# Attention and gated feed-forward on one core: seven half products for half of gate and value, a residual added by transfers, and a listed order

## The chip, the core and the metric

The kernel runs on one core of a Trainium2 chip. A core has a matrix engine (TensorE, PE in the profile), a vector engine (DVE), an activation engine (ACT), a general engine (POOL) and a queue engine (SP); POOL and SP issue the transfers here. Matmul results go to PSUM, eight banks of 128 x 512 fp32. The metric is device time in microseconds, the median of three runs.

## The reference, cut to what is computed

The first stage is attention over 4 batches, 8 heads, 768 positions and 64 values per head. Heads 0, 2 and 6 are causal; the other five see only the first 4 positions and the last 64. The second stage takes the result as x, 3072 tokens of 512 features:

```python
x = np.ascontiguousarray(attn_out.transpose(0, 2, 1, 3)).reshape(B * S, H * D)
g = x @ w_gate                                    # 512 -> 1536
gelu = 0.5 * g * (1.0 + erf(g * inv_sqrt2))
val = x @ w_val                                   # 512 -> 1536
ffn_out = gelu * val @ w_out                      # 1536 -> 512
res_gate = 1.0 / (1.0 + np.exp(-(x @ w_res)))
return (x + res_gate * ffn_out).astype(np.float32)
```

## The kernel before

The 3072 tokens are worked in six chunks of 512, c = 0 to 5 (the constant CHUNKS, line 25); a chunk may span two batches. For every chunk there is an attention stage (scores, exponentials, masks, weighted values, a transpose to features), a gate/value stage and an output stage. Work of neighbouring chunks overlaps: while gate and value of chunk c run, the output of chunk c-1 and the scores of chunk c+1 are fitted in.

Nothing is written as a loop of instructions. Functions add tasks to a graph (class Graph, line 195), each with an engine, a duration, what it depends on, a priority and its buffers. Tasks are numbered in the order in which they are added. `schedule` (line 219) then plays time forward and lets each free engine take the ready task of lowest priority number; HINTS (line 46) overrides single priorities by task number. `assign_waits` turns dependencies into semaphore waits and `emit` writes each engine's instructions in the order found. An engine executes its list in order, so a waiting instruction holds up all behind it. A task that has two homes (`flex`, line 212) goes to DVE or ACT as time is played.

Buffers come from pools. `P_ot` is four tiles otile of 128 x 512 fp32, `P_sr` three srs; `P_ps` is PSUM, with a list of permitted banks and a number held at once for each kind of use.

Gate and value (`gate_value`, line 1121): for each f of 12 blocks of 128 hidden features, gate and value are four matmuls each, with a 128 x 128 block of wg or wv as weights and 512 tokens of xT moving. ACT applies gelu (line 1166), DVE multiplies gelu and value into hT (line 1168). c=0 works the first blocks in halves of 256 tokens.

The output stage (`output_fast`, line 1213; the first half of c=0 uses `output`) already multiplies hT and wo by seven half products for a pair of token tiles, pi = 0 or 1, with sums of hT (`sums`, line 1174, line 1187) and of wo (`weight_sums`, line 1199, line 1204) made on DVE. Partial results are copied (keep, lines 1251 and 1252) and added (plus, line 1257) in otile; gated (line 1281) multiplies by the residual gate; then DVE, or POOL in c=5, adds x (line 1286), and SP stores the tile (line 1292). For c=5, pi=1 is called `end`.

Each matmul goes through `mm` (lines 513 to 517): where the tiling of PE is by columns, it is issued as two halves of 64 columns of weights (line 517), otherwise whole (line 516). q and k are loaded by POOL (line 577) and, from c=2 on, transposed by SP's transfers into one tile qkt that holds q and k of a whole batch.

Of the kernel before, what the change touches and what calls it, by code (L numbers as in the profile page):

```python
# [4 lines left out]
NHEAD = 8  # L5
SEQ = 768
DHEAD = 64
# [36 lines left out]


HINTS = (
    "3:-58.9 11:-130.04 428:854.14 430:718.61 444:2782.08 457:-821.9 460:407.45 490:4205.68 521:1522.06 "
    "591:-818.43 610:-36.63 612:486.89 613:-2965.25 619:1544.03 621:-44.07 643:467.87 644:-881 646:4.3 656:119.6 "
    "664:25.04 673:629.62 675:-109.25 695:-2674.26 696:-1856.67 703:-881.5 706:-108.75 707:714.39 708:1939.7 "
    "711:270.02 712:497.18 716:476.22 720:652.56 738:638.32 743:520.23 744:3053.24 749:514.3 750:1799.28 "  # L50
    "751:2383.53 756:521.28 762:1469.72 764:4344.87 767:2237.74 787:-603.93 815:5053.25 817:2978.67 821:1231.87 "
    "824:1484.86 836:2402.62 837:798.1 841:706.04 848:-288.52 849:2997.07 876:2751.74 906:2555.54 913:1516.93 "
    "918:2437.99 919:1519.88 924:1537.25 931:1510.23 936:2384.32 949:2443.79 955:2089.28 967:2846.74 995:-227.38 "
    "1001:29.83 1002:3171.86 1003:3180.29 1004:1146.58 1007:2686.58 1012:1781.89 1040:-803.29 1043:1907.45 "
    "1045:1028.83 1046:667.33 1050:3229.28 1051:1536.45 1053:3573.03 1056:-1823.77 1084:4090.27 1110:2454.97 "
    "1111:2597.62 1117:2808.38 1123:2507.5 1128:2481.58 1129:2529.63 1134:2508.5 1146:2434.73 1152:2779.33 "
    "1153:3034.61 1158:3861.94 1165:2795.06 1171:3076.63 1176:2997.8 1185:5989.69 1188:2243.92 1189:2528.84 "
    "1192:2789.39 1193:2537.45 1194:3836.22 1208:3021.15 1215:6294.68 1263:3219.13 1268:5037.38 1283:4420.5 "
    "1308:4756.92 1311:3513.6 1317:3517.03 1321:3052.3 1329:5930.49 1330:3507.5 1335:3508.5 1336:3519.22 "
    "1341:4624.14 1345:3444.6 1353:3516.64 1354:3538.83 1357:2761.66 1365:3787.63 1366:5173.04 1372:5102.72 "  # L60
    "1386:5438.32 1392:4014.31 1393:4933.66 1418:5146.68 1430:4133.91 1441:5428.8 1452:5127.54 1457:2188.42 "
    "1462:4595.33 1464:5711.23 1467:9389.54 1468:4425.54 ~1471:550.69 1476:5611.77 1499:4504.13 1513:6742.83 "
    "1516:5340.27 1522:4510.5 1523:4585.63 1526:3632.38 1534:4503.02 1539:4253.34 1550:4463.64 1565:7711.51 "
    "1570:4506.5 1571:5085.34 1580:2427.42 1594:2466.44 1610:9272.71 1625:3048.93 1627:6036.71 1629:6167.81 "
    "1631:5064.12 1644:6476.5 1662:4125.72 1671:5044.95 1672:7314.6 1676:4967.2 1683:6427.71 1692:9540.12 "
    "1711:7387.16 1757:5137.62 1784:5507.1 1797:5469.41 1803:7562.23 1817:7773.49 1818:7478.69 1823:7672.83 "
    "1834:7419.08 1836:10250.4 1849:7490.55 "
)

# [121 lines left out]
VS_DMA = 0  # L191
LAT = {"pe": 0.20, "act": 0.10, "dve": 0.08, "pool": 0.12, "sp": 0.1}


class Graph:
# [22 lines left out]

    def schedule(self):
# [21 lines left out]
        running = []  # L241
        while left:
# [3 lines left out]
            for e in ENGS:  # L246
# [3 lines left out]
                for t in cand[e]:  # L250
# [6 lines left out]
                    key = (int(away), p_, t.seq)  # L257
                    if t.ready > now or (best is not None and key >= bkey):
                        continue
                    if t.alts and any(max(free[f], now) + t.alts[f][0] + BIAS[f] < now + t.alts[e][0] + BIAS[e] - 1e-6  # L260
                                      for f in t.alts if f != e):
                        continue
# [22 lines left out]
                progressed = True  # L285
                if t.name == "g0" and warming:
                    warming = False
                    cand["pe"] = [w for w in cand["pe"] if w.name != "warm"]
                    gone = [w for w in self.tasks if w.name == "warm" and w.end is None]
                    left -= len(gone)  # L290
                    self.tasks = [w for w in self.tasks if w not in gone]
# [109 lines left out]
    def emit(self):  # L401
# [31 lines left out]
        with nc.Block() as blk:  # L433
# [17 lines left out]
            @blk.sync  # L451
            def _(e):
                run("sp", e)
                for t in finals:
                    e.wait_ge(t.sem, 16)
# [6 lines left out]
def c_act(n):  # L462
    return 0.19 + n * 0.000834


def c_dve(n, rate=1.0, psum=True):
    return (0.125 if psum else 0.065) + n * 0.00104 / rate
# [6 lines left out]
def build_kernel(nc, q, k, v, w_gate, w_val, w_out, w_res, out):  # L474
# [11 lines left out]
    scratch = sb("scratch", [128, 1], FP16)  # L486
    blank = sb("blank", [128, 128], FP16)
# [4 lines left out]
    P_vs = Pool(many("vs", 2, [128, NT - 1, NHEAD, DHEAD + 1], FP16))  # L492
    P_vk = Pool(many("vk", 2, [128, 8, DHEAD + 1], FP16))
    P_qkt = Pool(many("qkt", 2, [128, 2, NPAIR, SEQ], FP16))
# [9 lines left out]
    P_hs = Pool(many("hS", 1, [128, 3, NF // 2, 2, 128], FP16))  # L504
    wt = sb("wt", [128, 4, NF // 2, 256], FP16)
    P_ga = Pool(many("gact", 4, [128, 512], FP16))
    P_sr = Pool(many("srs", 3, [128, 512], FP32))
# [5 lines left out]
    def mm(e, o, lhsT, rhs, **k):  # L513
# [8 lines left out]
        "gv": (4, one(6, 7, 5, 4, 3, 2)), "gv0": (4, one(6, 7, 5, 4)), "gvh": (4, one(7, 6, 4, 5)), "out": (2, one(6, 7)), "fin": (4, one(6, 7, 1, 0)), "warm": (1, one(7, 5)),  # L522
# [55 lines left out]

    wtok = {}

    def load_weights():
# [6 lines left out]
        for j in range(4):  # L588
# [3 lines left out]
            wtok["o", j].late = 2.2  # L592
        for nm in "gv":
            for j in range(3):
                wtok[nm, j].late = 2.2 if j else 2.0
# [8 lines left out]
    def batch(b):  # L604
        if b not in batches:
            B_ = B()
            B_.v, B_.vs, B_.vk, B_.qkt = Buf(P_v), Buf(P_vs), Buf(P_vk), Buf(P_qkt)
# [4 lines left out]
        return batches[b]  # L612

    def values(b, a, z, base, each, on_engines=False):

        BB = batch(b)
        for i in range(a, z):
            BB.vtok[i] = dma("pool", base, 0.9, (lambda i=i: lambda: at(BB.v)[:, i, :, 0:DHEAD])(),
                             v[b, :, i * 128:(i + 1) * 128, :].rearrange("h p d -> p h d"), bufs=[BB.v])
            BB.vtok[i].late = 1.6 if base < 50 else 6.0  # L620
        if a == 0:
# [9 lines left out]
            for t in BB.vktok:  # L631
                t.slack = 12.0 if b else 0.0
# [5 lines left out]
        if on_engines:  # L638
            ts = []
            for lo, hi, pr in ((1, 2, -75),) + (() if VS_DMA else ((2, 4, 130),)):  # L640
                for dst, src, off in ((0, 64, 1), (64, 0, 0)):
                    def vs(on, dst=dst, src=src, off=off, lo=lo, hi=hi):
                        def fn(e):
                            o = at(BB.vs)[dst:dst + 64, lo - 1:hi - 1, :, :].rearrange("p i h d -> p (i h d)")
                            i_ = at(BB.v)[src:src + 64, lo - off:hi - off, :, :].rearrange("p i h d -> p (i h d)")
                            return e.activation(out=o, in_=i_, func=AF.Copy) if on == "act" else e.tensor_copy(out=o, in_=i_)
                        return fn
                    n_ = (hi - lo) * 520
# [9 lines left out]
        for lo in cuts:  # L658
            hi = lo + 1 if each else z
            ts = []  # L660
            for dst, src, off in ((0, 64, 1), (64, 0, 0)):
                ts.append(G.add("sp", 1.2, (lambda lo=lo, hi=hi, dst=dst, src=src, off=off: lambda e: e.dma_start(
                    at(BB.vs)[dst:dst + 64, lo - 1:hi - 1, :, :].rearrange("p i h d -> p (i h d)"),
                    at(BB.v)[src:src + 64, lo - off:hi - off, :, :].rearrange("p i h d -> p (i h d)")))(),
# [7 lines left out]
    def loads_rows(c, si, b, a, z):  # L672
# [27 lines left out]
        per = 1 if c == 0 or n == 4 else 2  # L700
        for k_ in range(0, NPAIR, per):
            ps_ = ORDER[k_:k_ + per]
            pr = 1000 * c - 492 + ps_[0] if c else 40 * k_ - 205
            for js in (((1,), (0,)) if c == 0 else ((0, 1),)):
                scr = Buf(P_ps, "scr" if c else "scr0")
                items = [(p, jj) for jj in js for p in ps_]
# [10 lines left out]
                def ev(on, p0=ps_[0], scr=scr, j0=js[0], m=len(items)):  # L717
                    def fn(e):
                        o = at(BB.qkt)[:, :, :, lo:hi].rearrange("c j (y x) w -> c x (j y) w", x=2)[:, p0 % 2]
                        m0 = j0 * 2 + p0 // 2  # L720
                        o = o[:, m0:m0 + m, :].rearrange("c m (p j) -> c m p j", j=n)
# [5 lines left out]
                           bufs=[scr, BB.qkt], name="qkE")  # L727
# [4 lines left out]
    def loads_natural(c, si, b, a, z):  # L732
# [8 lines left out]
        for i in range(a, z):  # L741
            for j, src in ((1, k), (0, q)):
# [11 lines left out]
                t = G.add("sp", 1.65, (lambda sv=sv, i=i, j=j: lambda e: e.dma_start(  # L754
# [690 lines left out]
```

The softmax here doesn't subtract the row's maximum and nothing guards it: scores larger than these inputs give would overflow.

## Time and profile before

| what | value |
|---|---|
| median of three runs | 265.71 us (265.57 to 266.54) |
| span of the profiled execution | 263.7 us |
| ACT gelu, line 1166 | 68 of 597 ns |
| DVE product, line 1168 | 68 of 686 ns |
| output transfers on SP, issue to landing | 2.4 us (median) |
| loads of v on POOL, issue to landing | 17.6 us (median) |
| PE clock granted | 1.000 |

The span is that of one profiled execution; the runs are timed without a profile. In the profile a group line gives count, total busy time and mean length of one instruction, then the idle time of the engine before them and what ended it. In a table of windows each pair is busy time and number of instructions, for PE, PEld (weight loads), DVE, ACT and POOL, then clock, transfer share and GB/s.

### The profile page before, as it was taken

The page shows a single profiled execution, that of the slowest core. Times are in us where ns is not written, and L with a number is a line of the kernel's source. Part 1 is how long each engine was busy: PE and PEld are TensorE (multiplying, and loading weights), DVE is VectorE, ACT ScalarE, POOL GpSimd, SP SyncE. Part 2 cuts the span into 40 slices and gives each one's busy share as a digit, 9 for nine tenths or more (in the row PEclk, how much of TensorE's full clock was granted, in tenths as well). Part 3 has the DMA queues.
Part 4 walks back from the last instruction along what each step waited for, and adds up shares of the span by engine and source line. Part 5 has one row for each costly group of instructions (what it writes and reads, how often), then busy time and mean ns, then how long its engine had stood idle before and what let it go on. Part 6 is the DMA issues. An engine that isn't in the chain of part 4 may idle for free.

```text
span 263.7 us, 7495 instructions
## 1 busy us (share of the span) xinstructions
PE 257.7 (98%) x3226; PEld 164.0 (62%) x3226; DVE 181.6 (69%) x378; ACT 147.2 (56%) x237; POOL 89.3 (34%) x127
## 2 busy tenths in 40 slices
PE   7999999999999999999999999999999999999993
PEld 6777655468444668544567444589655588655692
DVE  2698437798447888557898366888557689837655
ACT  2785467974244987423787242967243888233430
POOL 8999979506109973975000000000000000000003
PEclk9999999999999999999999999999999999999999
DMA  6999999999999999999996110004200004200003
GB/s 83 174 204 206 188 175 231 175 153 204 134 200 148 165 137 177 171 179 176 174 156 150 42 40 0 2 26 101 82 2 0 2 2 122 82 2 0 2 35 127
DMA packets 96513, 29.22 MB, mean 111 GB/s; under 512 B 84449, under 2 KB 93025, under 8 KB 96481
## 3 DMA queue, kind: packets, MB, share of 16 engines
q0 software_dynamic: 70320, 14.69, 67.5%
q1 hardware_dynamic: 26160, 14.07, 28.0%
q8 instruction: 25, 0.41, 0.7%
q14 instruction: 8, 0.06, 0.1%
HBM read 29.36 MB, written 6.29 MB: 135 GB/s over the span
## 4 chain that ended last, share of the span: by engine, by line
PE 95%; DMA 2%; DVE 1%; issue 0%; POOLq 0%
PE ps L516 50%; PE ps L517 32%; PE ps L893 5%; PE ps L1333 2%; PE ps L1017 2%; PE ps L709 2%; DMA qks<-in_q_dram 2%; PE ps L1106 2%; PE ps L984 1%; DVE otile L1281 1%; DVE otile L1286 1%; DVE otile L1257 0%; POOLq L1427 0%
## 5 line engine op out<-in xcount | busy, mean ns | idle before, releaser
L1166 ACT ACTIVATE gact<-ps 128x512 f16<-128x512 f32 x68 | 40.2, 597 | 73.5 <-PE ps L516 43.7
L1168 DVE SCALAR_TENSOR_TENSOR hT<-gact,ps 128x512 f16<-128x512 f16 x68 | 46.1, 686 | 48.0 <-PE ps L516 23.1
L516 PE MATMUL ps<-xT,wg 128*128 128x512 f16 (+1 forms) x208 | 50.0, 363 | 0.0
L516 PE MATMUL ps<-xT,wv 128*128 128x512 f16 (+1 forms) x202 | 49.0, 362 | 0.0
L1286 POOL TENSOR_TENSOR otile<-otile,xtok 128x256 f32<-128x256 f32 x3 | 2.4, 801 | 136.2 <-DVE otile L1281 136.2
L577 POOL DMA_DIRECT2D qks<-in_k_dram x36 | 28.0, 810 | 17.3 <-DMA qkt<-qks 13.9
L516 PEld LDWEIGHTS ps<-xT,wg 128*128 128x128 f16 x208 | 20.1, 98 | 20.0 <-DVE otile L1257 0.3
L516 PEld LDWEIGHTS ps<-xT,wv 128*128 128x128 f16 x202 | 19.4, 98 | 20.0 <-DVE hT L1168 0.5
L577 POOL DMA_DIRECT2D qks<-in_q_dram x36 | 28.4, 828 | 2.2 <-issue 1.4
L517 PE MATMUL ps<-xT,wv 128*64 128x512 f16 x204 | 28.3, 380 | 0.0
L577 POOL DMA_DIRECT2D va<-in_v_dram x24 | 21.3, 920 | 15.1 <-PE ps L516 15.1
L517 PE MATMUL ps<-xT,wg 128*64 128x512 f16 x192 | 26.3, 379 | 0.0
L909 ACT ACTIVATE ea<-ps 128x1024 f16<-128x1024 f32 (+2 forms) x24 | 21.1, 915 | 1.7 <-PE ps L893 1.6
L1257 DVE TENSOR_TENSOR otile<-otile,ps 128x256 f32<-128x256 f32 x33 | 13.6, 417 | 7.1 <-PE ps L517 4.7
L1226 ACT ACTIVATE srs<-ps 128x512 f32<-128x512 f32 x22 | 13.1, 595 | 9.1 <-PE ps L517 6.7
L517 PEld LDWEIGHTS ps<-xT,wv 128*64 128x64 f16 x204 | 11.5, 110 | 9.8 <-DVE hT L1168 0.3
L1084 DVE TENSOR_TENSOR xtok<-ps,rcp 128x512 f32<-128x512 f32 (+1 forms) x28 | 16.8, 606 | 0.2
L517 PEld LDWEIGHTS ps<-xT,wg 128*64 128x64 f16 x192 | 11.1, 110 | 9.0
L893 PE MATMUL ps<-qkt 64*128 64x64 f16 (+4 forms) x391 | 16.4, 213 | 0.0
L893 PEld LDWEIGHTS ps<-qkt 64*128 64x128 f16 x391 | 9.8, 94 | 8.0 <-issue 4.2
L516 PE MATMUL ps<-wo,hT 128*128 128x256 f16 (+1 forms) x84 | 14.4, 304 | 0.0
L1286 DVE TENSOR_TENSOR otile<-otile,xtok 128x512 f32<-128x512 f32 (+1 forms) x21 | 14.3, 691 | 0.2
(109 smaller groups left out, 437.4 us busy)
## 6 DMA issues: line engine op xcount, KB each, us to landing
out_dram<-otile SPq DMA_DIRECT2D x22, 256.0 KB, 2.4
va<-in_v_dram POOLq DMA_DIRECT2D x24, 128.0 KB, 17.6
qks<-in_k_dram POOLq DMA_DIRECT2D x32, 64.0 KB, 12.6
qks<-in_q_dram POOLq DMA_DIRECT2D x32, 64.0 KB, 13.0
wg<-in_moe_w_gate_dram POOLq DMA_DIRECT2D x3, 512.0 KB, 10.2
wv<-in_moe_w_val_dram POOLq DMA_DIRECT2D x3, 512.0 KB, 12.1
wo<-in_moe_w_out_dram POOLq DMA_DIRECT2D x4, 384.0 KB, 22.8
vs<-va SPq DMA_DIRECT2D x4, 260.0 KB, 7.9
```

Source lines behind the costliest of these rows:

```text
L516: return e.matmul(o, lhsT=lhsT, rhs=rhs, **k)
L517: return [e.matmul(o[h:h + 64], lhsT=lhsT[:, h:h + 64], rhs=rhs, **k) for h in (0, 64)][-1]
L577: return G.add(eng, issue, lambda e: e.dma_start(out_ap(), in_ap), deps, prio, bufs=bufs, dma=cost, name=name, grp=grp)
L709: return [e.transpose(out=at16(scr)[64 * x:64 * x + 64, (m * n + i) * 128:(m * n + i + 1) * 128], in_=piece(jj, h, i), identity=ident[:, : ...
L893: return [e.matmul(at(scr)[:, oo:oo + w], lhsT=side(BB, low, 1)[half, k0:k0 + 128], rhs=side(BB, low, 0)[half, qq:qq + w], start=True, sto ...
L909: return e.activation(out=o, in_=i_, func=AF.Exp, scale=SM_SCALE)
L1084: t2 = G.add("dve", c_dve(2 * n * 64), lambda e: e.tensor_tensor(out=xview(), in0=avv(0, DHEAD), in1=scale(), op=ALU.mult), [t1] + xdeps, ...
L1166: ta = G.add("act", c_act(512), (lambda gb=gb, ga=ga: lambda e: e.activation(out=at(ga)[:, :], in_=at(gb)[:, :], func=AF.Gelu))(), [tg], p ...
L1168: th = G.add("dve", c_dve(512), (lambda vb=vb, ga=ga, f=f: lambda e: e.scalar_tensor_tensor(out=hv(f), in0=at(ga)[:, :], scalar=0.5, in1=a ...
L1226: tas.append(G.add("act", c_act(512), (lambda rb=rb, sr=sr: lambda e: e.activation(out=at(sr)[:, :], in_=at(rb)[:, :], func=AF.Tanh, scale ...
L1257: return G.add("dve", c_dve(256), lambda e: e.tensor_tensor(out=dst(), in0=dst(), in1=at(D)[:, 0:256], op=ALU.add), [t, k], pr, bufs=[D, o ...
L1286: fn = (lambda ot=ot, lt=lt, w=w: lambda e: e.tensor_tensor(out=at(ot)[:, w], in0=at(ot)[:, w], in1=at(xbuf)[:, lt, w], op=ALU.add))()
```

## The change

Six things are changed.

1. From c=1 on, blocks f = 6 to 11 of gate and value are paired (6 with 9, 7 with 10, 8 with 11). For each pair and each of the two weights a unit of seven half products (`fast`) takes the place of eight matmuls of 512 columns. It works in a "lane" of two PSUM banks, freed by f = 0, 1 or 2 of the same chunk; there are three lanes. The products accumulate in the lane; between them one quarter is copied to another (seed), one is kept in an otile buffer (hold), and DVE adds twice (merge). Sums of x are made per chunk on DVE (`xS`), sums of the weights once (`gv_sums`).
2. The residual of c=1 to 5, except in the last pair (`end`), is added by transfers: SP stores x into the output (`store_x`), and POOL then sends each gated tile with accumulation.
3. A list PLAN gives each engine's order, in the sequence PE, ACT, DVE, POOL, SP; HINTS is empty. Tasks with two homes take the one whose list names them.
4. q and k have tiles of their own (kT per batch, qT per chunk), so the copy q6 becomes two transfers; the shifted copy vs leaves out head 0.
5. The fourth sum of wo and the third sums of wg and wv are written over the block that they replace. hS is split in two tiles, srs has two buffers.
6. Warm-up matmuls are 256 columns wide; the durations that `schedule` uses are changed.

```diff
+VS = (NHEAD - 1) * (DHEAD + 1)
+NP = 3
+FA, FB = NF - 2 * NP, NF - NP
+LANES = 3
...
+PLAN = (
+    "228 232 230 226 409 236 462 240 406 457 238 460 234 420 412 423 417 424 425 426 430 432 431 440 441 442 474 443 469 "
...
+    "1650 1651 1586 1660 1656 1657 1594 1595 1661 1658 1662 1659 1663 1590 1591 1667 1668 1669 1600 1601 1597 1598 1673 "
+    "1675 1606 1603 1604 1679 1607 1686 1697 1685 1680 1681 1691 1682 1693 1698 1687 1692 1694 1699 1688 1719 1700 1741 "
+    "1703 1730 1705 1722 1744 1704 1733 1724 1706 1725 1735 1746 1727 1736 1747 1749 1738 1710 1752 1709 1711 1755 1712 "
+    "1763 1774 1757 1766 1777 1758 1768 1769 1779 1760 1780 1771 1782 1822 1824 1826 1797 1827 1798 1799 1828 1829 1800 "
+    "1832 1803 1833 1804 1835 1806 1836 1838 1839 1807 1841 1842 1844 1809 1812 1813 1845 1810 1793 1795 1815 1816 / 198 "
...
+    "1721 1731 1743 1707 1732 1728 1729 1750 1753 1751 1713 1764 1775 1776 1772 1773 1825 1823 1801 1830 1802 1831 1678 "
+    "1834 1805 1794 1796 / 1 0 16 15 17 231 227 14 241 237 11 408 235 411 459 464 222 223 415 416 427 433 428 429 444 419 "
...
+    "327 392 399 298 321 324 301 323 305 306 317 330 315 314 299 341 302 326 874 348 358 318 871 345 359 900 356 340 335 334 "
...
+    "1347 1344 383 1373 1583 1376 1609 1612 1580 1848 1854 1849 1855 1818 1821 / 260 246 261 247 286 292 618 289 629 268 295 280 "
...
@@ schedule
+                offers = cand[e]
+                if queue:
+                    offers = [t for t in queue[e][heads[e]:heads[e] + 1] if t in offers] + [t for t in offers if t.name == "warm"][:1]
...
-    P_qkt = Pool(many("qkt", 2, [128, 2, NPAIR, SEQ], FP16))
+    P_kt = Pool(many("kT", 2, [128, NPAIR, SEQ], FP16))
+    P_qt = Pool(many("qT", 2, [128, NPAIR, 512], FP16))
...
+        "lane": (LANES, [(4, 5), (2, 3), (0, 1)]),
...
+    def gv_sums():
+        for nm, w in (("g", wg), ("v", wv)):
+            wt_ = gvt[nm]
+            blk = lambda k, j: w[:, 2 * k:2 * k + 2, (FB if j else FA) * 128:(FB if j else FA) * 128 + NP * 128]
+            here = [wtok[nm, j] for j in range(3)]
...
+            t1 = add(wt_[:, 0], blk(0, 1), blk(0, 0), here, 0)
+            t2 = add(wt_[:, 1], blk(1, 1), wt_[:, 0], [t1] + here, 1)
+            t4 = add(wt_[:, 2], blk(1, 0), wt_[:, 1], [t2] + here, 2)
+            t3 = add(blk(0, 1), blk(1, 1), blk(0, 1), [t1] + here + gv_tail, 3)
...
+    def fast(c, xtbuf, xttoks, h, toks, hv, lanes_):
...
+        s1 = add(lambda: S(0), lambda: A(1, 0), lambda: A(1, 1), ALU.add, xd, [xs, xtbuf])
+        s2 = add(lambda: S(1), lambda: S(0), lambda: A(0, 0), ALU.subtract, [s1] + xd, [xs, xtbuf])
+        s3 = add(lambda: xs3[:, :, :], lambda: A(0, 0), lambda: A(1, 0), ALU.subtract, xd + xs3_last, [xtbuf])
+        s4 = add(lambda: S(2), lambda: A(0, 1), lambda: S(1), ALU.subtract, [s2] + xd, [xs, xtbuf])
...
+        for q in range(2 * NP):
+            j, nm = q // 2, "gv"[q % 2]
...
+            lane = lanes_[q % LANES]
+            ps, free = lane
+            es = Buf(P_ot)
+            AL, AR, BL, BR = (slice(x * 256, x * 256 + 256) for x in range(4))
...
+            t15 = product([("A11", "B11", AL, True), ("S1", "T1", AR, False)], list(free))
+            seed = copy((lambda ps=ps: at(ps)[:, BL]), (lambda ps=ps: at(ps)[:, AL]), [t15], [ps], "seed")
+            hold = copy((lambda es=es: at(es)[:, 0:256]), (lambda ps=ps: at(ps)[:, AR]), [seed], [ps, es], "hold")
+            t6 = product([("S2", "T2", BL, False)], [seed])
+            m1 = merge(AR, [t6, hold])
+            t7 = product([("S3", "T3", BL, False)], [m1])
+            t23 = product([("A12", "B21", AL, False), ("S4", "B22", AR, False)], [m1])
+            m2 = merge(BR, [t7])
+            t4 = product([("A22", "T4", BL, False)], [m2])
...
+    def store_x(c, xbuf, xtoks):
+        n = 2 if c == len(CHUNKS) - 1 else 4
+        r0 = c * 512
+        stored[c] = G.add("sp", 0.65, lambda e: e.dma_start(
+            out[r0:r0 + n * 128, :].rearrange("(i p) d -> p i d", p=128), at(xbuf)[:, 0:n, :]),
...
@@ output_fast
+            if c >= ACCUM and not end:
+                t = G.add("pool", 1.0, (lambda ot=ot, r0=r0: lambda e: e.dma_start(out[r0:r0 + 128, :], at(ot)[:, :], accum_op=ALU.add))(),
+                          ends + [stored[c]], pr - 3000, bufs=[ot], dma=1.0, name="out")
+                t.late = 0.5
+                continue
```

In a unit, product multiplies the named sums of x (A and S) with the named blocks or sums of the weights (B and T) over 256 tokens, two matmuls for each; merge adds the held otile to BL and writes AR or BR.

## The prediction

> **What bounds the kernel now.** I read the page first: busy shares, the 40 slices, the chain that ended last.
>
> ```profile
> PE 257.7 (98%) x3226; PEld 164.0 (62%) x3226; DVE 181.6 (69%) x378; ACT 147.2 (56%) x237; POOL 89.3 (34%) x127
> PE   7999999999999999999999999999999999999993
> DMA  6999999999999999999996110004200004200003
> PE 95%; DMA 2%; DVE 1%; issue 0%; POOLq 0%
> ```
>
> TensorE (PE) is busy in every slice but the first and last and is 95% of the chain; transfers stop being dense after slice 22 (about 145 us). So a microsecond of PE work removed is worth up to a microsecond, if nothing else becomes late. Next, what one matmul costs. A busy share won't tell, since matmuls overlap; start to start in the timeline of PE does:
>
> ```profile
> 226.86 0.60 PE L517 MATMUL ps<-xT,wv 128*64 128x512 f16 x4
> 227.29 0.60 PE L517 MATMUL ps<-xT,wg 128*64 128x512 f16 x4
> ...
> 248.44 0.82 PE L517 MATMUL ps<-wo,hT 128*64 128x256 f16 x12
> 249.09 0.82 PE L517 MATMUL ps<-wt,hS 128*64 128x256 f16 x12
> ```
>
> L517 issues each matmul as two column halves that run side by side. Four records of 512 columns are two matmuls in 0.43 us, 0.215 each; twelve records of 256 columns are six in 0.65 us, 0.109 each. Half the columns cost half the time, and the weight loads stay hidden at 256. Third, the busy time by stage, whose columns are PE, PEld, DVE, ACT, POOL: a gate/value stage (225 to 247) beside an attention stage (205 to 225).
>
> ```profile
> 205.00:225.00 20.00, 20.00 (x468) 15.24 (x463) 16.34 (x37) 16.14 (x23) 0.00 (x0) 1.00 0.16 42
> 225.00:247.00 22.00, 22.00 (x218) 12.22 (x216) 13.62 (x23) 7.34 (x13) 0.00 (x0) 1.00 0.07 26
> ```
>
> DVE has 8 us free and ACT 15 in the gate/value stage; both are over 80% busy in attention. Last, the groups that give prices, and the end of the chain:
>
> ```profile
> L1168 DVE SCALAR_TENSOR_TENSOR hT<-gact,ps 128x512 f16<-128x512 f16 x68 | 46.1, 686 | 48.0 <-PE ps L516 23.1 <-ACT gact L1166 15.6 <-PE ps L517 8.9
> L1257 DVE TENSOR_TENSOR otile<-otile,ps 128x256 f32<-128x256 f32 x33 | 13.6, 417 | 7.1 <-PE ps L517 4.7 <-PE ps L516 2.0
> L1286 DVE TENSOR_TENSOR otile<-otile,xtok 128x512 f32<-128x512 f32 x20 | 13.4, 684 | 0.2
> L1252 ACT ACTIVATE otile<-ps 128x256 f32<-128x256 f32 x18 | 6.7, 380 | 5.5 <-PE ps L517 3.9 <-PE ps L516 1.5
> L1187 DVE TENSOR_TENSOR hS<-hT 128x512 f16<-128x512 f16 x6 | 2.6, 426 | 0.2
> 259.33 1.01 DVE otile L1281 x3
> 260.37 0.77 DVE otile L1286
> ```
>
> The last matmuls start at 259.2, DVE ends at 261.14, and the last transfer carries the span to 263.7.
>
> **What the Trainium skill says.** "TensorE: Matmul & The Clock Gate", Back-to-back issue gap: N/2.4 + 2.5 ns for one matmul of N columns, 109.2 and 215.8 ns; the two rates above agree (0.109, 0.215). "PSUM — Partial Sum Buffer", PSUM bank collisions: two engines must not touch one bank of a quadrant at once, so the copies and merges inside a new unit cannot lie beside its own matmuls; this trace shows no unit of that kind. "DMA: Bandwidth & Descriptors", SWDGE vs HWDGE vs iDMA: an accumulating transfer is issued by GpSimd only, which here means POOL's queue, the one that carries all loads. Same page, Two DMAs through the same engine are not ordered: within one queue of one DMA engine descriptors start in order, so it stands behind loads issued earlier; the trace shows what that can mean, loads of va landing 17.6 us after issue (median, the page's part 6) against 2.4 us for an output on SP.
>
> **The change part by part.**
>
> *Removed from PE.* From c=1 on, f 6 to 11 of gate and value become three pairs times two weights, six units in each of five chunks, 30 in all. A unit was 8 matmuls of 512 columns: 8 x 0.2158 = 1.726 us. It becomes seven products of two matmuls of 256 columns: 14 x 0.1092 = 1.529 us. 30 x 0.197 = **-5.9 us**, all of it on the path.
>
> *Added by the units.* Each unit is a chain: two products, seed and hold (copies of 256 columns), one product, merge, one product, merge, one product, then gelu or multiply. From the last issue slot of a product to its reader's start this trace shows about 0.27 us (product slot ends 249.75, L1252 starts 250.02), and I take 0.1 back to PE, so a copy holds the unit up for 0.27 + 0.38 + 0.1 = 0.75 us and a merge for 0.27 + 0.42 + 0.1 = 0.79. Other lanes and the plain f 3 to 5 are the cover. Counting tasks in order of creation I placed the end of the PE list for c=5: after the last plain matmul only units 3 to 5 remain (1752 to 1784), two of which wait for their seeds with 0.65 us of other work before them. Walking it through with these numbers leaves PE idle for about 0.1 + 0.2 us. Bounds: 0.1 a chunk if drains are shorter, 0.7 if DVE is a merge late. I take 0.32 a chunk, five chunks, **+1.6 us** (0.5 to 3.5).
>
> *DVE and ACT.* Merges 60 x 0.417 = 25.0 us on DVE. Sums of x, 4 x 5 x 0.42 = 8.4 (row L1187 of 512). Sums of the weights once, 8 of 768 columns, between the 0.43 of 512 and the 0.69 of 1024, so 0.55 each: 4.4, in c=0, before c=1's units need them. The 60 seeds and holds have two possible homes; in the lists of c=4 and c=5 ten of twelve are ACT's, so 50 x 0.38 = 19 us on ACT, 10 x 0.42 = 4.2 on DVE. Seeds read and write PSUM, which no row shows; between 0.2 and 0.42, I take L1252's 0.38. The adds of the residual go: 18 of L1286, 12.3 us. DVE becomes 181.6 + 25.0 + 8.4 + 4.4 + 4.2 - 12.3 = 211 us, ACT 166, both under a span near 260. In the stage 225 to 247, DVE was 13.6 of 22; less two adds (1.4), plus 1.7 + 5.0 + 0.8, it is 19.7 of about 21. It is covered by PE, but nearly full: a late h or merge then has no slack. I cost it at nothing beyond the 1.6; if the cover is gone, it is the second rival.
>
> *Residual by transfers.* SP now stores x (1 MB per chunk, half in c=5) as soon as attention is done, and 18 tiles leave POOL as accumulating transfers, each about 0.9 us of POOL (row of va, 920 ns) and waiting for the store and for gated. Behind a waiting one on POOL stand later loads. In the trace those end their issue at 122 us, while q, k and v of the last chunks are used from about 165, so 40 us hide a delay. After 145 us transfers have room. At the very end the old tail was 4.2 us from the last matmul's slot (259.5) to the span's end. The new POOL list ends 1848 1854 1849 1855 1818 1821: the pair formerly first (pi=0) now ends last. After PE: 0.4 to DVE, two gated of 0.42 less overlap (0.8), POOL's 0.95, then landing and close, 2.1 + 0.4 as on SP: 4.7, and up to 6 if the read-modify-write lands later. **+0.7 us** (-0.3 to +1.8).
>
> *Smaller edits.* q and k get tiles of their own, q6 two transfers instead of one, vs copies 456 of 520 columns, srs two buffers: under transfers that landed early or on engines with idle time, taken as 0 together (-0.5 to +0.5). Warm-up matmuls are as long as before in sum.
>
> *The fixed order.* Summing every matmul record from 20 us to the last start at its issue cost (column halves as half, row halves as half) gives 228.1 of 239.2 us: 11 us are lost, mostly in the attention stages and their two ends. A list can give some back, or lose more where durations differ. Bounds -4 and +2; I take a fifth of the loss, **-2.1 us**. This is my choice, not a reading.
>
> Sum against the profiled execution: 263.7 - 5.9 + 1.6 + 0.7 - 2.1 = 258.0 us of span; the median of 265.71 lies 2.0 above that span, which I carry over: **260.0 us**.
>
> **The rivals.** *More comes back* (chance 0.17): DVE rid of 12 us of adds at the ends of chunks, where attention has it over 80% busy, so the boundary losses shrink by 4 and units stall by 0.5: 263.7 - 5.9 + 0.5 + 0.7 - 5 + 2.0 = 256.0. For it: the losses sit at those boundaries. Against it: merges give DVE more than it loses.
> *DVE becomes the second bound in gate/value* (0.14): 19.7 of 21 us with waits in order; half a microsecond more a chunk from late merges, half a microsecond of h late into the output products, and no gain by order: 260.0 + 2.5 + 1.0 = 263.5. Against it: ACT takes most copies.
> *It comes to nothing* (0.06): both of the above at once, 265.7.
> *Slower: tiles held by accumulating transfers* (0.13). The hold of a unit uses the pool otile, four buffers, which the four output tiles of the chunk before hold until they have landed. Until 145 us DMA is full, and behind the loads on POOL's ring an accumulate could take the 13 us of the loads of q and k. Outputs of c=1 leave at 96 to 109 us, c=2's units start near 113: the hold has no buffer, PE stops. Five us at each of the handovers c=1 to 2 and c=2 to 3: 260.0 + 10 = 270. It decides from 2.9 us each. For it: the loads' landing times. Against it: the list interleaves only few loads between the accumulates.
> That the change does not do its work: a seed counts only if the next matmul adds to it; by the PSUM page's four rules it does where an earlier matmul wrote those columns, which the plain value product of the lane has done; time is the same either way.
>
> **How the numbers follow.** The forecast 260.0 has 0.50, its own range 257.5 to 262.5 (units 0.5 to 3.5, tail, order). With 256.0 (0.17) and 263.5 (0.14) the range 254.8 to 265.2 leaves out the slower case, most of no change and a little below. Faster by over 0.5% (below 264.4; about what a measurement of this kernel can tell from none): 0.81; within: 0.06; slower: 0.13.
>
> **What would show it.** Right (two column halves counted as one): 420 more matmuls of 256 columns on wg, wv and their sums, 240 fewer of 512; their start to start near 0.109; PE still over 90% of the chain; DVE 205 to 215 us; 60 merges near 0.42. Wrong: idle of PE before products released by a merge or a seed over 1 us a chunk; an accumulate landing over 8 us after its issue before 145 us with a hold waiting for it; a tail over 6 us after the last matmul.

## The result, and the profile after

| | before | changed |
|---|---|---|
| median, same chip | 265.64 us (4 runs) | 269.37 us (4 runs, 269.22 to 270.07) |
| ratio, 95% interval | 1 | 1.0134 (1.0116 to 1.0152) |
| span of the profiled execution | 263.7 us | 267.4 us |

The forecast was 260.0 us with a range up to 265.2: the change makes the kernel slower by 1.3%. (Of all kernels below only b1 had most of its runs, three of four, at a lower granted clock, so its time is not compared with others.) The page of the changed kernel, in the order in which the page before was read (busy shares, slices of PE and of the transfers, engines of the chain):

```profile
PE 254.3 (95%) x3428; PEld 181.7 (68%) x3428; DVE 200.9 (75%) x447; ACT 166.1 (62%) x297; POOL 106.6 (40%) x146
PE   7999999999999999979999999999999999999970
DMA  6999999999999999999999996505680026720026
PE 82%; DMA 8%; DVE 4%; POOL 2%; issue 2%; ACT 0%; POOLq 0%; DVEq 0%
```

PE still is the bound, but its share of the chain fell from 95 to 82%: DMA, DVE and POOL now hold 14%. There is a hole in slice 18 of PE (near 118 us), the last slice is empty, and transfers are dense to slice 24 in place of 21. PE itself got its gain. In PE's timeline of the changed kernel, units and plain matmuls of c=5 stand side by side:

```profile
233.23 0.41 PE L591 MATMUL ps<-xT,wg 128*64 128x256 f16 x4
233.45 0.41 PE L591 MATMUL ps<-wS,wgt 128*64 128x256 f16 x4
233.66 0.62 PE L591 MATMUL ps<-xT,wv 128*64 128x512 f16 x4
234.10 0.41 PE L591 MATMUL ps<-xT,wg 128*64 128x256 f16 x4
```

Two matmuls of 256 columns (four records of column halves) take 0.22 us from start to start, two of 512 take 0.44: half the columns cost half the time. So I sum all matmul records at their issue cost, as in the prediction (warm-up matmuls at nothing), now stage by stage, and take the rest of each stage as lost. A stage of c ends with the last matmul of c's gate and value; it holds the output of c-1, attention of c, and gate/value of c. "Start" is everything to the end of c=0's gate and value, "tail" runs from the last matmul's start to the span's end. All in us:

| kernel | PE work | start | c=1 | c=2 | c=3 | c=4 | c=5 | output | tail | span |
|---|---|---|---|---|---|---|---|---|---|---|
| before | 233.5 | 15.9 | 2.0 | 2.0 | 2.3 | 2.2 | 1.1 | 0.1 | 4.4 | 263.7 |
| changed | 227.6 | 17.6 | 1.8 | **4.7** | **3.3** | 1.9 | 2.1 | 0.0 | **8.4** | 267.4 |

The work fell by 5.9 us, and 9.7 us more are lost: 4.0 in the tail, 2.7 in c=2, 1.7 in the start, 1.0 in c=3 and 1.0 in c=5, less 0.7 in the other places together. Three pieces of the chain of waits of the changed kernel show what PE waited for in c=2, in c=3 and at the end. At the handover of c=1 to c=2:

```profile
109.59 8.59 DMA out_dram<-otile
...
118.20 0.39 ACT otile L1336
...
118.69 0.45 DVE ps L1340
...
119.18 0.83 PE ps L590 x6
```

An accumulating transfer issued at 109.59 lands 8.59 us later; only then is its otile free, so that ACT can take the hold of a unit (line 1336), DVE merge (1340) and PE go on: the hole of slice 18. From PE's starts and issue costs this is one stop of 2.1 us. Before gate and value of c=3:

```profile
142.41 7.22 DMA xT<-x
149.64 0.05 issue
149.68 1.47 PE ps L590 x6
```

The transposing transfer that makes xT takes 7.22 us (3.4 at this place before), and PE stops for 0.8 us. And the end, where the chain leaves PE for ACT, DVE and POOL:

```profile
257.83 0.61 ACT srs L1437
...
258.46 0.70 DVE otile L1493
...
259.70 0.87 POOL out_dram L1497
260.58 0.87 POOLq L503
```

The issue of the last accumulating transfer starts at 260.5, 1.4 us after the last matmul's start; it lands 5.1 us later, at 265.6, and the span ends at 267.4. The group of these transfers (count, busy time, mean; idle time of POOL before them and what ended it) and their median from issue to landing:

```profile
L1497 POOL DMA_DIRECT2D out_dram<-otile x18 | 16.2, 957 | 81.1 <-DVE otile L1493 74.8
out_dram<-otile POOLq DMA_DIRECT2D x18, 256.0 KB, 5.3
```

POOL stands idle for 81 us in front of them, 75 of it until gated is done. Only two loads stand behind its waits of over 5 us, one of k issued at 150.36 and one of v at 188.17; all others were out by 144. The theory to test was that the transfers, not the units, make the loss; the rivals were the listed order and stalls inside the units.

### The profile page after: what moved, and what is told of

Same layout as the page of the kernel before. It is cut to its first block, busy times and chain, and to the rows that moved or that the text cites. A ratio compares the mean times of both kernels' runs of the same rounds, so it can differ in the third digit from the quotient of the medians.

```text
span 267.4 us, 8080 instructions
## 1 busy us (share of the span) xinstructions
PE 254.3 (95%) x3428; PEld 181.7 (68%) x3428; DVE 200.9 (75%) x447; ACT 166.1 (62%) x297; POOL 106.6 (40%) x146
## 4 chain that ended last, share of the span: by engine, by line
PE 82%; DMA 8%; DVE 4%; POOL 2%; issue 2%; ACT 0%; POOLq 0%; DVEq 0%
PE ps L590 39%; PE ps L591 30%; PE ps L987 5%; DMA out_dram<-otile 3%; DMA xT<-x 3%; PE ps L1552 3%; PE ps L1111 2%; PE ps L798 2%; DMA qks<-in_q_dram 2%; PE ps L1200 1%; DVE hT L1365 1%; PE ps L1078 1%; POOL out_dram L1497 1%; POOL va L652 1%; DVE hS L1388 1%
## 5 line engine op out<-in xcount | busy, mean ns | idle before, releaser
L1497 POOL DMA_DIRECT2D out_dram<-otile x18 | 16.2, 957 | 81.1 <-DVE otile L1493 74.8
L590 PE MATMUL ps<-xT,wg 128*128 128x512 f16 (+1 forms) x172 | 38.5, 337 | 0.7 <-DMA xT<-x 0.7
L590 PE MATMUL ps<-xT,wv 128*128 128x512 f16 (+1 forms) x168 | 37.9, 336 | 0.2 <-DVE hT L1238 0.2
L1340 DVE TENSOR_TENSOR ps<-ps,otile 128x256 f32<-128x256 f32 x60 | 24.4, 430 | 10.0 <-ACT otile L1336 4.0
L590 PEld LDWEIGHTS ps<-xT,wg 128*128 128x128 f16 x172 | 16.3, 98 | 11.3 <-DMA xT<-x 1.2
L591 PE MATMUL ps<-xT,wv 128*64 128x512 f16 (+1 forms) x152 | 19.6, 346 | 0.0
L590 PE MATMUL ps<-wo,hT 128*128 128x256 f16 (+1 forms) x114 | 19.2, 296 | 0.2 <-DVE hT L1388 0.2
L591 PE MATMUL ps<-xT,wg 128*64 128x512 f16 (+1 forms) x144 | 18.3, 344 | 0.0
L987 PE MATMUL ps<-qT,kT 64*128 64x64 f16 (+4 forms) x391 | 16.4, 213 | 0.0
L591 PE MATMUL ps<-wo,hT 128*64 128x256 f16 x216 | 15.2, 273 | 0.0
```

Of the source, the lines that this page charges most:

```text
L590: return e.matmul(o, lhsT=lhsT, rhs=rhs, **k)
L591: return [e.matmul(o[h:h + 64], lhsT=lhsT[:, h:h + 64], rhs=rhs, **k) for h in (0, 64)][-1]
L987: return [e.matmul(at(scr)[:, oo:oo + w], lhsT=side(BB, qb, low, 1)[half, k0:k0 + 128], rhs=side(BB, qb, low, 0)[half, qq:qq + w], start=T ...
L1340: return G.add("dve", c_dve(256), lambda e: e.tensor_tensor(out=at(ps)[:, o], in0=at(ps)[:, BL], in1=at(es)[:, 0:256], op=ALU.add), deps, ...
L1497: t = G.add("pool", 1.0, (lambda ot=ot, r0=r0: lambda e: e.dma_start(out[r0:r0 + 128, :], at(ot)[:, :], accum_op=ALU.add))(), ends + [stor ...
```

## The experiments

Line numbers in these kernels lie 13 to 20 above those of the changed kernel (e8 keeps them), in b1 at least 77 above those of the kernel before. ADDS names the chunks whose residual is added by an engine again (with an output on SP and no store of x); MOVES takes a task behind another in the list of one engine. Each row of the table shows losses in us as above; PE's work is 227.6 in all of them, and the output loses 0.0 to 0.6. Each row is one profiled execution: up to c=4 the lists of e1 are those of the changed kernel, and its c=1 still lost 0.7 us more, at one stop for a late copy vs, so a single difference of that size proves nothing:

| kernel | time, us | ratio (95%) | start | c=1 | c=2 | c=3 | c=4 | c=5 | tail | span |
|---|---|---|---|---|---|---|---|---|---|---|
| e1 | 266.18 | 0.9995 (0.998 to 1.001) | 17.7 | 2.5 | 4.5 | 3.1 | 1.9 | 2.1 | 4.5 | 264.5 |
| e2 | 269.28 | 1.0114 (1.0063 to 1.0165) | 17.7 | 1.8 | 3.6 | 2.9 | 1.9 | 2.6 | 7.7 | 266.3 |
| e3 | 265.29 | 0.9974 (0.9953 to 0.9996) | 18.3 | 1.8 | 3.5 | 2.7 | 2.3 | 2.3 | 4.6 | 263.5 |
| e5 | 264.68 | 0.9944 (0.9928 to 0.996) | 17.0 | 2.4 | 4.1 | 2.7 | 2.3 | 2.3 | 4.5 | 263.4 |
| e6 | 268.36 | 1.0089 (1.0057 to 1.0121) | 17.6 | 1.8 | 2.8 | 3.1 | 1.9 | 2.5 | 8.1 | 266.0 |
| e8 | 264.10 | 0.9924 (0.9904 to 0.9944) | 17.7 | 1.8 | 2.7 | 2.5 | 1.9 | 2.1 | 5.7 | 261.8 |
| e9 | 263.99 | 0.9918 (0.9892 to 0.9944) | 16.8 | 1.8 | 3.4 | 2.7 | 2.3 | 2.3 | 4.6 | 262.0 |
| e10 | 264.27 | 0.9919 (0.9893 to 0.9946) | 17.3 | 1.8 | 2.6 | 2.9 | 1.9 | 2.3 | 4.5 | 261.5 |

### e1: the last two accumulating transfers replaced

```diff
+ADDS = (5,)
...
+            if c in ADDS and not end:
+                t = G.add("dve", c_dve(512), (lambda ot=ot, lt=lt: lambda e: e.tensor_tensor(
+                    out=at(ot)[:, :], in0=at(ot)[:, :], in1=at(xbuf)[:, lt, :], op=ALU.add))(), ends + xtoks[lt], pr, bufs=[ot, xbuf], name="add")
+                G.add("sp", 0.6, (lambda ot=ot, r0=r0: lambda e: e.dma_start(out[r0:r0 + 128, :], at(ot)[:, :]))(),
+                      [t], pr - 3000, bufs=[ot], dma=0.75, name="out", extra=True).late = 0.5
+                continue
```

> The two tiles of c=5, pi=0 get their residual by DVE adds and leave on SP; all else is the changed kernel. Transfer theory (the end of the span is 4 us longer because the last accumulating transfers land 5 to 7 us after their issue on POOL): the time from the last matmul to the end of the span falls from 8.4 to about 4.5 us and the time from 269.4 to 265.5 to 266.5. Rival (units and DVE carry the loss, the end would be as late with adds): 268.5 or more, the adds standing in DVE's way.

Measured: 266.18 us, no different from before (0.9995) and as the transfer theory had it; the tail fell from 8.4 to 4.5, nearly what it was before the change. Two of 18 transfers carry 3 us: they stand at the end, where nothing follows that could cover them.

### e2: the transfers of c=1 replaced

```diff
+ADDS = (1,)
```

> Only the four tiles of c=1 get their residual by DVE adds and leave on SP; c=2 to 5 as in the changed kernel. Transfer theory (hold of a unit of c=2 waits for an otile that an accumulating transfer of c=1 keeps for 8.6 us): the wait of ACT for out_dram is gone, PE's loss in c=2 falls by 2 to 2.7 us, the time is 266.7 to 267.5. Rival (DVE too full in gate/value): the four adds of 0.69 us on DVE make it 269 to 271.

Measured: 269.28 us with runs from 267.97 to 270.75: the median lies in the rival's range, but is too scattered to tell from the changed kernel. The span is 1.1 us shorter. The wait for otile is gone and with it PE's stop of 2.1 us, but c=2 lost only 1.1 less (3.6 in place of 4.7), where 2 to 2.7 was expected. A stop of 0.8 us that the changed kernel doesn't have stands in its chain:

```profile
105.51 0.42 DVE otile L1482
105.93 0.35 DVE xT L1221
106.28 0.05 issue
106.32 0.40 PE ps L1213 x4
```

PE waits for DVE's copy into xT. All kernels that add the residual of c=1 on DVE (e2, e3, e5, e9) have this stop, and none of the others. So the held tile is most of what c=2 lost to the change, and adds on DVE take part of it back, as the rival said. A second place where DVE is late is in every kernel with units (here e10):

```profile
125.67 1.28 DVE hT L1378 x2
126.95 0.48 DVE hS L1401
...
127.47 1.30 DVE hT L1378 x2
...
130.76 0.60 DVE hS L1401
131.36 0.35 DVE hT L1401
...
131.82 1.47 PE ps L603 x12
```

At the end of c=2's gate and value DVE is behind: products of units and sums of hT follow each other for 6 us (in the changed kernel DVE is busy 5.86 of the 6 us from 128 to 134), and the chain runs through DVE before it returns to PE's output products. PE has other work meanwhile and stops only 0.4 us at the end of it, which the table counts in c=3. That is the prediction's second rival, DVE as the bound, in one place and small.

### b1: accumulating transfers alone

The kernel before, without units, its own order written out as a list, with the transfers of point 2 of the change.

```diff
+ACCUM = (1, 2, 3, 4, 5)
...
+            if c in ACCUM and not end:
+                t = G.add("pool", 1.0, (lambda ot=ot, r0=r0: lambda e: e.dma_start(out[r0:r0 + 128, :], at(ot)[:, :], accum_op=ALU.add))(),
+                          ends + [stored[c]], pr - 3000, bufs=[ot], dma=1.0, name="out")
```

> The kernel before in its own order on PE, ACT and DVE, with the residual of c=1 to 5 by stores of x and accumulating transfers, but for the last pair; no units. Theory that the transfers hurt only where something waits for their landing (otile of the holds, the end): nothing waits here, 264.5 to 266.5. Rival (the added traffic itself delays loads and xT): 267 to 270.

Measured: 282.31 us (275.46 to 286.19) beside 266.22; only the places of its waits are read here. Its chain of waits:

```profile
119.21 18.53 DMA qks<-in_q_dram
...
151.05 6.64 DMA xT<-x
157.69 0.05 issue
157.74 2.31 PE ps L593 x5
```

My expectation fell, its rival was nearer. A load of q took 18.53 us to land (the last eight before, 12 to 16), SP's transposes waited for such loads, and xT queued behind those on SP. PE waited 7.0 us for it. POOL stood 123.5 us before accumulating transfers, but only 4.8 of that came before its last load, at 128 (121 before): the loads were late mostly in landing. Whether traffic or the transfers in front of them in the queue made them so, this run doesn't tell. The order here is that of the kernel before with the transfers put in, not the changed kernel's, so the size says little; the way does.

### e3: no accumulating transfers at all

```diff
+ADDS = (1, 2, 3, 4, 5)
```

DVE takes an add whenever the head of its list isn't ready; SP takes an output as soon as it is ready.

> The changed kernel with all residuals of c=1 to 5 added by DVE where the head of its list is not ready, outputs on SP, no stores of x. Transfer theory alone: both losses go, 4 + 2.7 us, 262.5 to 264. Rival (DVE is the second bound; 18 adds of 0.69 us in a list made without them): 266 to 271, with PE waiting for merges and sums.

Measured: 265.29 us, 0.9974, between the theory (262.5 to 264) and its rival (266 to 271): units and list, without the transfers, are slightly faster than before and 1.6% faster than the changed kernel. The waits for otile and xT's transfer are off the chain; DVE's 0.8 us stop of e2 is in it.

### e5: the start

```diff
+MOVES = (('pe', 250, 528),)
```

> All residual adds on the engines as in e3, and one task moved in PE's list: the group of 16 transposes of the second chunk's q, at 20.6 us, goes behind the first three gate products. Theory (the list loses time at the start because a group of transposes that waits for a late load stands in front of matmuls that are ready): the first gate product starts at 20.0 to 20.5 us in place of 21.7, and the time falls 1.0 to 1.8 us below e3's, to 263.5 to 264.3, ratio to before 0.990 to 0.995. Rival (the start is set by x, its transposes and the weights, the transposes only fill a hole): the first gate product stays at 21.5 or later, time 265.0 to 265.5. Second rival: the transposes are then late for the second chunk's scores, and the gain is lost before 60 us.

Measured: 264.68 us; its interval overlaps that of e3. The start lost 17.0 in place of 18.3, but c=1 and c=2 lost 0.6 and 0.7 more, and the span stayed (263.4). The first gate product came at 21.1 (22.4 in e3), between the theory's 20.5 and the rival's 21.5. The gain was lost, as in the second rival, but not to late transposes; the chain says to what:

```profile
42.01 10.27 DMA va<-in_v_dram
...
52.30 7.49 DMA vs<-va
...
80.76 0.34 SPq L1529
...
83.37 8.03 DMA q<-qT
```

A load of va was late, so was SP's copy made from it, and PE stopped 0.7 us for that at 59.8; a copy of q stood on SP behind an output (L1529), which waited for DVE, and PE stopped 0.6 us for it at 91.7. The first stop, though, is also in e1, where nothing of this was moved.

### e6: two loads behind the third transfer

```diff
+MOVES = (('pool', 345, 900), ('pool', 359, 345))
```

> The changed kernel with two loads (one of k, 256 KB, and one of va) moved behind the third accumulating transfer on POOL, nothing else. Theory A (the 8.6 us of landing at 109.59 come from the loads issued just in front on the same queue): the third transfer lands in 4 to 6 us, the wait of 2.6 us for otile at 118 us falls to 0.5 or less, loss at the handover of c=1 to 2 about 1 us smaller, time 268.0 to 269.0. Theory B (an accumulating transfer takes this long under any load of the DMA engines): landing stays above 7 us, time 269.0 to 270.0. Rival: the two loads, later by about 4 us, make something else late in c=3, time above 270.

Measured: 268.36 us, ratio 1.0089, an interval that just meets the changed kernel's. The transfer issued at 109.57, third of its kind, and what ACT still waited for a tile:

```profile
out_dram<-otile POOLq DMA_DIRECT2D x1, 256.0 KB, 6.7
  DMA out_dram<-otile: 0.7, 1
```

Landing 6.7 us, between the two theories (4 to 6, over 7) where 8.6 was before; the wait fell from 2.6 to 0.7, c=2 lost 1.9 less, the span is 1.4 shorter. So the loads issued just in front made up some 2 us of the landing. The Trainium skill's "DMA: Bandwidth & Descriptors", Two DMAs through the same engine are not ordered, says that descriptors of one queue start in order, and this trace agrees; the rest is the transfer's own, or from other traffic.

### e8: plain stores in place of accumulation

```diff
-e.dma_start(out[r0:r0 + 128, :], at(ot)[:, :], accum_op=ALU.add)
+e.dma_start(out[r0:r0 + 128, :], at(ot)[:, :])
```

> The changed kernel with the 18 accumulating transfers as plain stores on the same queue at the same places, so that the residual of c=1 to 5 is left out of those tiles. Theory A (the read, add and write of the accumulation makes the landing long): landing falls from 5.3 us median to 2 to 3, the tail from 8.4 to 5.5 to 6.5 us after the last matmul's start, the wait for otile at 118 us is gone, time 265.5 to 267.5. Theory B (the queue of POOL is what is slow, not the addition): landing stays at 4.5 us or more, time 268.5 to 270.0.

Measured: 264.10 us, 2.1% below the changed kernel with the same lists, queue, bytes stored and places, and below the theory's 265.5. Its transfers, and its end of the chain:

```profile
out_dram<-otile POOLq DMA_DIRECT2D x18, 256.0 KB, 3.7
```
```profile
255.56 0.70 DVE otile L1493
...
256.81 0.56 POOL out_dram L1497
257.36 0.18 issue
257.54 0.57 POOLq L503
```

The median landing is 3.7 us in place of 5.3, an issue occupies POOL 0.55 us in place of 0.90 (medians), the last store lands in 2.4 us where the accumulation took 5.1. The wait for otile is gone and xT's transfer is off the chain. The span falls by 5.6 us: 2.7 in the tail, 2.1 in c=2, 0.8 in c=3. This is the experiment that decides: the addition in the transfer is what costs most of the loss. The tail stays 1.2 longer than before, with POOL's queue in the place of SP's. The median landing stays above the 2 to 3 us that theory A asked for; whether that is POOL's queue or other traffic isn't separated (SP's own outputs of 256 KB, all before 92 us, took 4.1 us in this kernel).

### e9 and e10: what a mended version gives

e9 is e5 with late transfers moved forward; e10 keeps accumulating transfers for c=1 to 4 with the same moves and those of e6.

The edit of e9, and then that of e10:

```diff
+ADDS = (1, 2, 3, 4, 5)
+MOVES = (('pe', 250, 528), ('sp', 660, 297), ('pool', 244, 208), ('pool', 255, 244), ('pool', 245, 255))
```
```diff
+ADDS = (5,)
+MOVES = (('pe', 250, 528), ('sp', 660, 297), ('pool', 244, 208), ('pool', 255, 244), ('pool', 245, 255), ('pool', 345, 900), ('pool', 359, 345))
```

> e5 (all residual adds on the engines, one group of transposes moved) with four more tasks moved in the lists: three loads of va go ahead of a load of q that waits on POOL for the transposes of PE until 37 us, and one output of c=0 on SP goes behind the two copies of q that it holds up until 83 us. Theory (e5 gave its start back because transfers of the second and third chunk are late, shown by DMA va<-in_v 10.27, vs<-va 7.49 and q<-qT 8.03 in its chain): losses of c=1 and c=2 fall from 2.36 and 4.13 to about 1.8 and 3.2, time 0.8 to 1.5 us below e5's, 263.2 to 263.9. Rival (PE is bound there by DVE's and ACT's work, the transfers only look late in the chain): the time stays within 0.4 us of e5's 264.7.

> The changed kernel, accumulating transfers kept for c=1 to 4, with everything found so far mended in the lists: the last two tiles of c=5 added on the engines, the two loads behind the third accumulate, the transposes of the start, the three loads of va and the output of SP moved as in e9. Theory (accumulating transfers cost only where something waits for their landing: the end, one otile, and xT of c=3 by traffic): tail 4.5 us, loss of c=2 about 2.5, start about 17; against the changed kernel -3.5 -1.9 -0.7, so 263.0 to 264.0 and as fast as e9 within 0.7. Rival (they cost everywhere, through traffic and POOL's queue): slower than e9 by over 1 us, 264.8 or more.

Measured: 263.99 and 264.27 us, ratios 0.9918 and 0.9919, both faster than before and than the changed kernel. In e9 c=1 and c=2 lost 1.8 and 3.4, near what was expected; the gain on e5, 0.7 us, is a little less than the 0.8 asked for, and the two intervals overlap. In e10 the four accumulating transfers of a chunk cost no more than DVE's adds: c=2 lost 2.6 where e9 lost 3.4, the difference being DVE's stop of 0.8 us, which e10 doesn't have; but xT of c=3 is late again:

```profile
139.93 6.79 DMA xT<-x
146.72 0.05 issue
146.76 3.41 PE ps L603 x15
```

## Why the prediction was wrong, step by step

The changed kernel's span is put together from e8 and the table, before rounding: 263.66 - 5.95 (PE's work) + 1.78 (start) + 1.18 (c=1 to 5, as e8 shows them) - 0.11 (output) + 6.88 (residual) = 267.44. The last term is the 5.64 us that e8 saves and the 1.24 us by which its tail is still longer than before; by places it is 4.0 in the tail, 2.1 in c=2 and 0.8 in c=3. It is the price against leaving the addition out. Against adds on DVE in the same list, which cost something themselves, it is 3.9 (267.4 - 263.5, e3).

*The step that failed is "residual by transfers", +0.7 (-0.3 to +1.8).* It measured +6.9, and three of its parts fell.
- Landing. I priced it "2.1 + 0.4 as on SP". At the end the last accumulation landed after 5.1 us, and the span ended another 1.8 us later. The tail was forecast at 4.7, up to 6; it was 8.4. The 1.8 are also in e8 and so not the addition's: where SP's transfer lands last, 0.5 us follow, and the 1.3 between are the part of the tail that plain stores on POOL keep. My own upper end, a late read and write, was set too low with no reading behind it: neither an accumulating transfer nor a store on POOL's queue was in the trace.
- "40 us hide a delay". The loads of q and k were issued to 151 us, not 122, and a last one of v at 188.17; in e3, without the accumulating transfers, all were out by 139. So units and list took some 17 us of the cover, and POOL's waits for gated the rest. PE waited for none of these loads, and in e8 they were as late (148 and 185) without harm. What I left out is that transfers still ran when xT of c=3 was made: with accumulation its transfer took 7.2 us and PE lost 0.8.
- The hold. I gave this a rival of its own, 10 us at two handovers, and the rival's time, 270, is near what was measured. But its mechanism appeared once, as a wait of 2.6 us and a stop of PE of 2.1 at c=1 to c=2, and not at c=2 to c=3. A landing of 8.6 us, under the 13 of the rival, was enough. That the time agrees is luck: the tail, which the rival did not contain, makes up for the rest.

Two of the prediction's signs of being wrong came, the landing over 8 us with a hold waiting and the tail over 6. Two of its rivals are summed wrongly. "No gain by order" alone gives back 2.1 us, which 260.0 + 2.5 + 1.0 has no room for; and both of the first rivals at once make 260.0 - 4.0 + 3.5 = 259.5, not 265.7.

*The fixed order, -2.1, was a choice and got the sign wrong.* The start lost 1.7 us more; e5 takes 1.3 from e3's start by moving one group of transposes from in front of gate products, and e9, where the transfers come earlier, keeps it. Even with these moves the start loses 0.9 more than before; how much of that is order isn't shown. No stage shows a gain over 0.4 us, and PE's timeline before says why there was little to gain (count is last):

```profile
139.97 0.82 PE L516 MATMUL ps<-wo,hT 128*128 128x256 f16 x6
140.62 0.82 PE L516 MATMUL ps<-wt,hS 128*128 128x256 f16 x6
141.37 0.22 PE L1017 MATMUL ps<-va,es 128*64 128x65 f16 x2
```

Six matmuls take 0.65 us to the next six, but 0.75 to matmuls that use PE in another tiling (128*64, two halves of columns, after 128*128). Counted in this way over all of c=1 to 5, PE starts 0.09 to 0.14 us late at each of 67 changes of tiling, 6.7 of the 9.7 us lost there. The list has 65 changes, and again 6.7 us. So most of the loss that I hoped to shorten is not idle time between late and early tasks, and an order shortens it only by having fewer changes.

*Right: PE's work*, -5.9 forecast, 233.5 - 227.6 = 5.9 measured, with 420 matmuls of 256 columns more and 240 of 512 fewer, as forecast. *Right in size, in part by luck: stalls of the units*, +1.6: c=1 to 5 lose 1.2 more than before in e8 and 1.8 in e10, which includes what order did there. Stops in front of products of units are only 0.6 us of e8's, in c=2, c=4 and c=5; 0.4 is the DVE stretch after c=2. In c=5, which loses 1.0 to 1.5 more in every kernel with units, 12 changes of tiling in place of 8 make up half, and no stop in the changed kernel or e8 is over 0.2 us.

*DVE and ACT.* ACT was forecast at 166 us and is 166.1; merges take 430 ns (forecast 417); seeds and holds went 50 to ACT and 10 to DVE, as the lists of two chunks had suggested. DVE was forecast at 211 and is 200.9. I added lengths of instructions to a busy time in which overlaps count once: the lengths alone sum to 198.2 before and 223.1 after, +24.9 where I had 29.4. The stage that I used for the second bound has more room than forecast (windows of the changed kernel; columns PE, PEld, DVE, ACT):

```profile
225.00:247.00 22.00, 21.98 (x314) 17.62 (x312) 16.47 (x36) 11.46 (x24) 2.54 (x3) 1.00 0.31 61
```

DVE is busy 16.5 of 22 us there, not 19.7 of 21, and 16.4 of the 21 us of c=2's stage from 113 to 134. So neither of these stages is full as a whole, though DVE is in the 6 us at the end of c=2's. Whether the order of its work makes that stretch, or sums and products that fall together, stays open: neither was tried.

Had an accumulation cost no more than a plain store (e8, 264.10 us), the time would have lain under 265.2, but only just and above the forecast's own 262.5: the optimistic order and the longer tail remained.

## What to carry to other kernels

An accumulating transfer is not a store plus a free addition: price its landing by itself, and put none where nothing follows, or where the tile that it reads is soon needed. In a queue that runs in order, a transfer that waits for late work delays all loads behind it; look for the first load that is behind it, and for what it will then run beside, not for the mean slack of the loads. A new listed order deserves no gain in advance: find out first what the lost time consists of. Moving one task pays only if the transfers that come next are early enough too.

## What the runs showed of the hardware

- Accumulating 256 KB on POOL's queue: 5.3 us median to landing (3.9 to 8.6), 5.1 for the last one with no load left; plain stores from the same places 3.7 (2.3 to 5.8), the last one 2.4; on SP, half as much (128 KB), 1.8 at the end of the kernel before. One issue occupies POOL 0.90 us with accumulation, 0.55 without (medians).
- From the last landing to the span's end 1.8 us where it is on POOL's queue (changed kernel, e2, e6 and e8, so with accumulation and without), 0.5 where it is on SP's (before, e1, e3, e5, e9 and e10).
- A change of PE's tiling between two matmuls cost 0.09 to 0.14 us of issue each of 67 times in c=1 to 5 of the kernel before; between matmuls of one tiling the median was nothing.
- The transposing transfer of xT near 140 us took 3.4 us before, 4.4 to 4.9 without transfers of the residual (e3, e5, e9), 5.8 with plain stores on POOL (e8), and 6.8 to 7.2 with accumulation. Other traffic is the likely reason, but it wasn't tested, and the next such transfer, near 180 us, shows no such order (3.2 with accumulation, 5.9 in e8).
